# Tile 1's decay sums and exponentials emitted ahead of tile 0's norm, its decays loaded from the input, and a scheduler that keeps column groups apart

## The chip, the cores and the metric

One core of one Trainium2 chip runs the kernel. The metric is the device time of one execution in microseconds (us), median of the runs shown. Names of engines: PE is TensorE (PEld its weight loads), DVE is VectorE, ACT is ScalarE, POOL is GpSimd, SP is SyncE, which here issues most of the DMAs.

## The reference

Three layers follow each other on a batch of 4 sequences of 768 positions. First a decaying state-space attention with 8 heads, computed chunk by chunk:

```python
L = np.exp(cum[:, :, :, None] - cum[:, :, None, :]) * causal   # cum: running sum of log(clip(a))
M = einsum('bhin,bhjn->bhij', Cc, Bc) * L
y = einsum('bhij,bhjd->bhid', M, xc) + einsum('bhin,bhnd->bhid', Cc, state) * exp(cum)
state = exp(sum(la)) * state + sum_j(B_j x_j * exp(cum[-1] - cum))
```

Then an FFN with a norm: `xn = x / sqrt(mean(x*x) + 1e-6) * rms_g`, `(silu(xn @ w_gate) * (xn @ w_val)) @ w_out`, 256 to 1536 to 256. Then a second FFN: each position is mixed with the one before it, `relu(xk @ w_k)**2 @ w_v` times `sigmoid(xr @ w_r)`, 256 to 1024 to 256. The weights arrive as 64-bit floats.

## The kernel before

The sequence is cut into six tiles of 128 positions. A tile holds these positions of all 4 sequences, so its matrices are 512 columns wide (T). The kernel runs a software pipeline over t from 0 to 5: in round t it computes the first FFN of tile t (`ffn1`, twelve units u of 128 hidden columns), the attention of tile t+1 between these units (`attend`), and the second FFN of tile t-1 (`ffn2`). Every large product is three matmuls (lines 670 to 672), a high part and a low part of each operand, so one unit of `ffn1` is 6 matmuls for g, 6 for v and 6 for x.

Weights are converted on the chip. `convert` (from line 246) takes two loaded pieces from a staging tile (`wst`, two buffers) and makes float pairs of them. On DVE that is L265, L270 and L272 on 1024 columns and two subtractions L282; on ACT it is L260, L261 and two casts L281. The pieces come in the order gate, val, out for two units at a time. The conversions for `ffn1` run during round 0, so round 0 has both the matmuls and the conversions.

The attention's decay matrix E exists in two forms. For tiles 0 and 1 it is computed as an exponential: `logs_e` takes the logarithms, `sums_e` (line 340) makes running sums and spreads them over helper operands in the weight tiles `wkh` and `wvvh` (DVE lines 342 to 352), `spread_e` (line 357) makes differences on PE in a PSUM tile Eb (a matmul with `eye`, then one with the sums), and `exp_e` takes exponentials on ACT into E, eight of 512 columns for a tile (E has four buffers, one for each sequence). Later tiles use a scan over decays that were stored to device memory (`la_r`, `la_d`). Independent of that, `la` holds running products of the decays of a tile; `la_scan` (L413) makes them and `ch_mul` (L417) scales C by them. In the kernel before, `decays` writes the clipped decays of all tiles to `la_d`, and `load_la` reads them back for every tile from tile 1.

Before round 0 the code emits: tile 0's sums, exponentials, scores, masks M and outputs y, then the norm of tile 0 (`norm0`: `rms_a` on ACT, `rms_b`, matmuls L646, `xn_f` L652 and `xn_split` L137 and L140), 24 matmuls that keep PE busy (`warm`, L801), the first two conversions, and tile 1's sums. Tile 1's exponentials follow inside round 0, from unit 0, by the table `SCAN`.

The order on each engine is not the emitted one. `Order` (line 998) replays the emitted instructions with a cost table: every engine takes the earliest emitted instruction that is ready, and a tile's buffer has to be free. `arrange` then fixes the resulting order on each engine. Each engine runs its instructions strictly in that order, so an instruction that is not ready holds up those behind it. What counts as ready there depends on `region`, which takes each access as a range of columns.

Of the kernel before, what the change touches and what calls it, by code (L numbers as in the profile page):

```python
# [9 lines left out]
F32 = mybir.dt.float32  # L10
# [6 lines left out]
P = 128  # L17
NB, NH, S, D, N = 4, 8, 768, 32, 16
# [3 lines left out]
T = NB * P  # L22
# [8 lines left out]

SCORES = ((4, 5, 7, 9), (2, 4, 7, 9), (2, 5, 8, 10))
VALUES = ((5, 7, 8, 10), (4, 6, 9, 11), (4, 7, 10, 12))
SCAN = ({0: (0, 1, 2, 3), 3: (4,)}, {0: (0,), 1: (4,), 3: (1,), 5: (2,), 7: (3,)})

NEED = ((6, 6, 6, 10, 10, 12, 12, 14, 16, 16, 18, 18, 18),
        (99, 99, 99, 99, 99, 99, 99, 99, 99, 99, 99, 99, 99))
# [39 lines left out]
def tile_kernel(ctx: ExitStack, tc, a_c, x_t, B_t, B_s, C_s, B_p, C_p, C_h, kc,  # L77
# [110 lines left out]
    def load_a():  # L188
        a_sb = t2("a_sb")[:NC * NR]
        nc.sync.dma_start(out=a_sb, in_=rows4(a_c.rearrange("c r i -> (c r i)")))  # L190
        return a_sb
# [108 lines left out]
    Sf = wp.tile([P, NB, NH // 2, D], F32, name="Sf")  # L300

    def load_la(c):
        t = A[c]["la"] = rp.tile([P, NB, P + 1], F32, tag="la", bufs=2, name="la")
        nc.gpsimd.memset(t[:, :, 0:1], 0.0)
        for b in range(NB):
            nc.sync.dma_start(out=t[:, b, 1:], in_=la_d[c, b].unsqueeze(1).broadcast_to([NH, N, P]))

    def load_ch(c):
        t = A[c]["Ch"] = rp.tile([P, NB, P], F32, tag="Ch", bufs=1, name="Ch")
# [46 lines left out]

    def spread_e(c, b):
        for half in range(2):
            pool, tag = (patt, "at") if c else (pmm, "mm")
            ps = A[c]["Eb", b, half] = pool.tile([P, T], F32, tag=tag, name="Eb")  # L360
            nc.tensor.matmul(ps, eye, before.unsqueeze(1).broadcast_to([P, 4, P]), start=True, stop=False)
            nc.tensor.matmul(ps, spread_l[c][:, 2 * b + half], spread_r[c].rearrange("p h i -> p (h i)"),
                             start=False, stop=True)
# [450 lines left out]
    for _ in range(2):  # L814
        w_load()
    first, second = steps(), steps()
    a_sb = load_a()
    for c in range(2):
        logs_e(c)
    def norm0(s):  # L820
# [5 lines left out]
            xn_split(0, half, s, act_e, vec_e)  # L826

    sums_e(0)
    for b in range(NB):
        spread_e(0, b)  # L830
        for half in range(2):
            exp_e(0, b, half)
    scores(0, 0)
    scores(0, 1)
    for b in range(NB):
        masked(0, b)
        if b + 2 < NB:
            scores(0, b + 2)
        y_mm(0, b)
        y_out(0, b)  # L840
        if b % 2:
            rms_sq(0, cols[b // 2], act_e, vec_e)
            rms_mm(0, cols[b // 2])
        st_up(0, b)
    for s in cols:
        norm0(s)
    warm_up(WARM[1], pacc, "acc")
    for step in first + second:
        step()
    sums_e(1)  # L850
    clip(a_sb)
    decays(a_sb)
    mu_rest()
    carry[0] = rp.tile([P, 2, NB], F32, tag="carry", bufs=2, name="carry")
    nc.vector.memset(carry[0], 0.0)
# [13 lines left out]
    for t in range(NC):  # L869
        c, e = t + 1, t + 2  # L870


        def exps(c, b):
            spread_e(c, b)
            for half in range(2):
                exp_e(c, b, half)

        def late(u):
            for b in SCAN[t].get(u, ()):
                if b == 4:  # L880
                    la_scan(c)
                    ch_mul(c)
                elif c == 1:
                    exps(c, b)
                else:
                    e_scan(c, b)

        def finish(b):
            if b % 2:
                y_two(c, b - 1)  # L890
                for k in range(b - 1, b + 1):
                    if e < NC:
                        load_e(e, k)

        at_sc, at_y = SCORES[min(t, 2)], VALUES[min(t, 2)]

        def attend(u):
            if t <= 1:
                late(u)
            elif u == 0:  # L900
                ch_mul(c)
            if u in (0, 3, 6, 8):
                bc(c, (u + 1) // 3)
            if u in at_sc:
                scores(c, at_sc.index(u))
                masked(c, at_sc.index(u))
            if u in at_y:
                finish(at_y.index(u))
            if u == NU and e < NC:
                load_ch(e)  # L910
                load_x(e)
            if e < NC:
                if u == 4:
                    load_la(e)
                elif u == 7 and t > 1:
                    e_scan(e, 0)
                elif u == 9 and t:
                    la_scan(e)
                elif u == 11 and t > 1:
                    e_scan(e, 1)  # L920
            if t == 0:
                if u == MEANS[0]:
                    rms_sq(c, cols[0], act_e, vec_e)
                if u == MEANS[0] + 1:
                    rms_mm(c, cols[0])
                if u == MEANS[1]:
                    rms_sq(c, cols[1], act_e, vec_e)
                    rms_mm(c, cols[1])
                    rms_a(c, full)

        def hook(kind, u):
            if kind == "ab":
                if t == 0:
                    need(NEED[0][u])
                    if u == 0:
                        for b in range(NB):
                            sf_up(0, b)
                if t == 1:
                    need(NEED[1][u])
                    if u == MIX_UNIT:  # L940
                        mix(0, held.pop(0), act_e, vec_e)
                elif t > 1 and u == 0:
                    mix(t - 1, held.pop(t - 1), act_e, vec_e)
                if c < NC:
                    attend(u)
            if kind == "cd2":
                tail()
            if kind == "cd" and c < NC:
                if t == 1 and u in (1, 2):
                    e_scan(e, u - 1)  # L950
                if u == 0:
                    rms_sq(c, full, act_e, vec_e)
                elif u == 3:
                    rms_mm(c, full)
                    rms_a(c, full)
                elif u == 4:
                    rms_b(c, full)
                    if e < NC:
                        e_scan(e, 2)
                elif u == 5:  # L960
                    xn_out(c, (0,), full, act_e, vec_e)
                    if e < NC:
                        e_scan(e, 3)
                elif u == 6:
                    xn_out(c, (1,), full, act_e, vec_e)

        x2, tail = ffn1(t, hook)
        if t == 0:
            tail()
            hook("ab", NU)  # L970
            rms_b(c, full)
            xn_out(c, range(2), full, act_e, vec_e)
            x2s = quad("x2s", F32).rearrange("p i a n -> p (i a n)")[:, :2 * NB * (P + 1)]
            x2s = x2s.rearrange("p (m b i) -> p m b i", m=2, b=NB)
            nc.gpsimd.memset(x2s[:, :, :, 0:1], 0.0)
            for m in range(2):
                nc.scalar.copy(x2s[:, m, :, 1:], x2[m].rearrange("p (b i) -> p b i", b=NB))
            x2 = [x2s[:, m] for m in range(2)]
        else:
            hook("ab", NU)  # L980
            ffn2(t - 1, hook)
        held[t] = x2
# [22 lines left out]
class Order:  # L1005
    SIGNAL, LANDING, RATE = 90.0, 1900.0, 270.0

    def __init__(self, instructions, slots, chains, groups):
# [13 lines left out]
        self.tiles, self.touch = [[] for _ in range(n)], {}  # L1022
        writes, reads = {}, {}
        for k, i in enumerate(self.ins):
            rs, ws = ([self.region(a, slots) for a in s if hasattr(a, "bass_ap")] for s in (i.ins, i.outs))
            for name in [name for name, _ in rs + ws] + groups.get(i.name, []):
                if name in slots and name not in self.tiles[k]:
                    self.tiles[k].append(name)
                    self.touch.setdefault(name, []).append(k)
            for name, r in rs:  # L1030
                self.meet(k, r, writes.get(name, ()))
            for name, r in ws:
                self.meet(k, r, writes.get(name, ()))
                self.meet(k, r, reads.get(name, ()))
            for store, them in ((writes, ws), (reads, rs)):
                for name, r in them:
                    if slots.get(name, ("",))[0] == "PSUM":
                        store = writes
                    store.setdefault(name, []).append((r, k))
# [1 line left out]


    @staticmethod
    def region(a, slots):
        ap = a.bass_ap
        steps = list(ap.ap)
        row = max(1, steps[0][0])
        at = ap.offset % row
        if ap.tensor.name.startswith("la_") or slots.get(ap.tensor.name, ("",))[0] == "PSUM":
            return ap.tensor.name, (0, 1 << 40, 0, P, None)  # L1050
        end = at + sum((c - 1) * max(s, 0) for s, c in steps[1:]) + 1
        size = 2 if ap.tensor.dtype == BF16 else 4
        return ap.tensor.name, (at * size, end * size, ap.offset // row, ap.offset // row + steps[0][1],
                                at % 2 if steps[-1][0] == 2 else None)

    def meet(self, k, r, others):
        for q, j in others:
# [184 lines left out]
```

## Time and profile before

| | us |
|---|---|
| median of 3 runs | 531.06 (529.59 to 533.97) |
| profiled execution, its time | 531.4 |
| its span, first to last instruction | 529.2 |
| PE busy | 517.0 (98%) |
| DVE busy | 397.5 (75%) |
| ACT busy | 310.3 (59%) |

The profile page has the busy time of each engine and the span in 40 slices of 13.2 us. The views of the trace used below are the stretches (busy time of each engine between two moments, the granted clock of PE and the share of the DMA engines), the waits (who waited for whom), and the timeline (instructions in order of time, equal neighbours merged, with the idle time before them in brackets). Durations in the timeline include the instruction's latency, so neighbours overlap a little; start to start is the rate.

### The profile page before, as it was taken

What the parts mean: (1) busy time and instruction counts of PE and PEld (TensorE: products, weight loads), DVE (VectorE), ACT (ScalarE), POOL (GpSimd) and SP (SyncE); (2) the same over time, 40 slices, a digit from 0 to 9 for tenths busy, and PEclk for the clock granted to TensorE, in tenths of its full rate; (3) what the DMA queues carried; (4) which work ended last, traced back from release to release, by engine and by line L of the source; (5) the groups of instructions that cost most, each with busy time, mean ns of one, the idle gap of its engine ahead of it and who ended that gap; (6) DMA issues with size and microseconds to landing.
All of it is one profiled execution on the core that took longest, in us unless ns stands there. A gap on an engine that the chain in (4) does not pass through costs nothing.

```text
span 529.2 us, 7538 instructions
## 1 busy us (share of the span) xinstructions
PE 517.0 (98%) x2872; PEld 417.4 (79%) x2872; DVE 397.5 (75%) x641; ACT 310.3 (59%) x507; POOL 14.1 (3%) x28
## 2 busy tenths in 40 slices
PE   9968999999999999999999999999999999999997
PEld 5746777888778888888888888788888888888885
DVE  5898999999999686688986587986445863335772
ACT  4768668755747974455874455774437663245552
POOL 4000000000002000001000001000000000000000
PEclk9998999999999999999999999999999999999999
DMA  7837445435334011325011324011000010000001
GB/s 217 276 108 214 170 165 185 154 90 158 111 99 142 19 41 51 109 71 168 20 41 48 112 64 155 2 40 41 0 1 1 0 40 1 1 1 0 22 19 40
DMA packets 21923, 42.34 MB, mean 80 GB/s; under 512 B 2096, under 2 KB 5168, under 8 KB 21888
## 3 DMA queue, kind: packets, MB, share of 16 engines
q1 hardware_dynamic: 19584, 33.48, 19.4%
q10 hardware_dynamic: 2304, 8.39, 4.7%
q8 instruction: 22, 0.36, 0.3%
q14 instruction: 13, 0.11, 0.1%
HBM read 38.52 MB, written 3.34 MB: 79 GB/s over the span
## 4 chain that ended last, share of the span: by engine, by line
PE 69%; DVE 2%; ACT 1%; POOL 0%; ACTq 0%; issue 0%; DVEq 0%
PE v L672 8%; PE v L670 8%; PE v L671 8%; PE g L670 4%; PE x L671 4%; PE x L672 4%; PE x L670 4%; PE g L671 4%; PE g L672 4%; PE kp L670 4%; PE kp L672 4%; PE kp L671 4%; PE y L504 1%; PE sc L472 1%; PE rps L671 1%; PE rps L672 1%
## 5 line engine op out<-in xcount | busy, mean ns | idle before, releaser
L701 DVE TENSOR_TENSOR hf<-sl,v 128x512 f32<-128x512 f32 x72 | 49.1, 682 | 48.9 <-PE v L672 45.7
L137 ACT CAST h<-hf 128x512 fp32r<-128x512 f32 x72 | 44.5, 619 | 65.2 <-DVE hf L701 65.1
L125 ACT ACTIVATE sl<-g 128x512 f32<-128x512 f32 x72 | 42.6, 593 | 44.3 <-PE g L672 44.3
L140 DVE TENSOR_TENSOR h<-hf,h 128x512 fp32r<-128x512 f32 x72 | 50.2, 700 | 23.4 <-ACT h L137 23.3
L670 PE MATMUL g<-xn,wgh 128*128 128x512 f32 x144 | 57.8, 403 | 0.8 <-ACT sl L125 0.8
L670 PE MATMUL v<-xn,wvh 128*128 128x512 f32 x144 | 56.6, 394 | 0.5 <-ACT sl L125 0.5
L671 PE MATMUL g<-xn,wgl 128*128 128x512 f32 x144 | 56.8, 395 | 0.0
L672 PE MATMUL g<-xn,wgh 128*128 128x512 f32 x144 | 56.7, 394 | 0.0
L672 PE MATMUL v<-xn,wvh 128*128 128x512 f32 x144 | 56.4, 392 | 0.0
L671 PE MATMUL v<-xn,wvl 128*128 128x512 f32 x144 | 56.4, 392 | 0.0
L670 PE MATMUL x<-h,woh 128*128 128x512 f32 x144 | 56.2, 390 | 0.0
L671 PE MATMUL x<-h,wol 128*128 128x512 f32 x144 | 56.1, 390 | 0.0
L672 PE MATMUL x<-h,woh 128*128 128x512 f32 x144 | 55.8, 390 | 0.0
L140 DVE TENSOR_TENSOR h<-k,h 128x512 fp32r<-128x512 f32 x48 | 32.8, 685 | 11.6 <-ACT h L137 11.0
L774 DVE TENSOR_TENSOR k<-rl 128x512 f32<-128x512 f32 x40 | 29.7, 748 | 14.7 <-ACT rl L770 14.5
L137 ACT CAST h<-k 128x512 fp32r<-128x512 f32 x48 | 29.8, 621 | 15.8 <-DVE k L774 15.5
L670 PE MATMUL kp<-xm,wkh 128*128 128x512 f32 x96 | 37.7, 393 | 0.0
L672 PE MATMUL v<-h,wvvh 128*128 128x512 f32 x96 | 37.5, 390 | 0.1
L672 PE MATMUL kp<-xm,wkh 128*128 128x512 f32 x96 | 37.4, 390 | 0.0
L670 PE MATMUL v<-h,wvvh 128*128 128x512 f32 x96 | 37.4, 389 | 0.0
L671 PE MATMUL kp<-xm,wkl 128*128 128x512 f32 x96 | 37.3, 389 | 0.0
L671 PE MATMUL v<-h,wvvl 128*128 128x512 f32 x96 | 37.3, 389 | 0.0
(148 smaller groups left out, 1027.8 us busy)
## 6 DMA issues: line engine op xcount, KB each, us to landing
E<-la_r ACTq DMA_DIRECT2D x16, 512.0 KB
x<-in_x_t SPq DMA_DIRECT2D x6, 512.0 KB
wst<-in_w_gate SPq DMA_DIRECT2D x6, 512.0 KB
wst<-in_w_val SPq DMA_DIRECT2D x6, 512.0 KB
wst<-in_w_out SPq DMA_DIRECT2D x6, 512.0 KB
Br<-in_B_s SPq DMA_DIRECT2D x12, 256.0 KB
Cr<-in_C_s SPq DMA_DIRECT2D x12, 256.0 KB
out<-r SPq DMA_DIRECT2D x12, 256.0 KB
```

The source lines that it names most:

```text
L125: ins.append(lambda: nc.scalar.activation(out=out, in_=in_, func=func, **kw))
L137: nc.scalar.copy(x[:, 0, :], src)
L140: last[0] = le.tensor_tensor(out=x[:, 1, :], in0=src, in1=f32(x[:, 0, :]), op=ALU.subtract).ins
L472: nc.tensor.matmul(bank[half][:, q * 256:(q + 1) * 256], bs[:, p, :], cs[:, p, :, :].rearrange("p a i -> p (a i)"), start=True, stop=True)
L504: nc.tensor.matmul(y[half][32 * j:32 * j + 32, at[half]:at[half] + P], x[:, b, h * D:(h + 1) * D], m[:, h, :], start=start and at[half] == ...
L670: nc.tensor.matmul(ps, w[0][:, k, ws], x[:, 0, :], start=first, stop=False)
L671: nc.tensor.matmul(ps, w[1][:, k, ws], x[:, 0, :], start=False, stop=False)
L672: nc.tensor.matmul(ps, w[0][:, k, ws], x[:, 1, :], start=False, stop=last)
L701: nc.vector.tensor_mul(hf, sl, v)
L774: nc.vector.tensor_mul(k2, rl, rl)
```

## The change

Five edits go together. `sums_e(1)` is emitted ahead of tile 0's masks, the exponentials of tile 1 for sequences 0 and 1 ahead of the norm of tile 0, and for 2 and 3 behind the first conversion; their PSUM tiles now come from the pool with four banks. The table `SCAN` loses the entry that placed them in round 0. Tile 1's decays are loaded straight from the input and clipped on DVE (four sequences, 128 columns each); the tile is named `decay` now. The stored decays for the later tiles are loaded, clipped and written in unit 2 of round 0. In the scheduler, `region` becomes `regions`: an access whose outer free dimension has up to 8 separate groups of columns is taken as several ranges.

```diff
-SCAN = ({0: (0, 1, 2, 3), 3: (4,)}, {0: (0,), 1: (4,), 3: (1,), 5: (2,), 7: (3,)})
+SCAN = ({3: (4,)}, {0: (0,), 1: (4,), 3: (1,), 5: (2,), 7: (3,)})
...
-            nc.sync.dma_start(out=t[:, b, 1:], in_=la_d[c, b].unsqueeze(1).broadcast_to([NH, N, P]))
+            src = la_d[c, b] if c > 1 else a_c[c, NH * b:NH * b + NH]
+            nc.sync.dma_start(out=t[:, b, 1:], in_=src.unsqueeze(1).broadcast_to([NH, N, P]))
+        if c == 1:
+            clip(t[:, :, 1:])
...
-            pool, tag = (patt, "at") if c else (pmm, "mm")
-            ps = A[c]["Eb", b, half] = pool.tile([P, T], F32, tag=tag, name="Eb")
+            ps = A[c]["Eb", b, half] = pmm.tile([P, T], F32, tag="mm", name="Eb")
...
-    a_sb = load_a()
...
     scores(0, 0)
     scores(0, 1)
+    sums_e(1)
     for b in range(NB):
         masked(0, b)
...
+    exps(1, 0)
+    exps(1, 1)
     for s in cols:
         norm0(s)
+    for step in first:
+        step()
+    exps(1, 2)
+    exps(1, 3)
     warm_up(WARM[1], pacc, "acc")
-    for step in first + second:
+    for step in second:
         step()
-    sums_e(1)
-    clip(a_sb)
-    decays(a_sb)
...
-                elif c == 1:
-                    exps(c, b)
...
+                if u == 2 and t == 0:
+                    a_sb = load_a()
+                    clip(a_sb)
+                    decays(a_sb)
...
-    def region(a, slots):
+    def regions(a, slots):
...
+        starts, free = [at], steps[1:]
+        inner = sum((c - 1) * max(s, 0) for s, c in free[1:]) + 1
+        if len(free) > 1 and free[0][1] <= 8 and free[0][0] > inner:
+            starts, free = [at + k * free[0][0] for k in range(free[0][1])], free[1:]
```

The first place is PE from tile 0's norm to the first units of round 0. `ss` is the norm's sum and its spread, `Eb` tile 1's differences, g and v are unit 0's products. Before:

```order
L801 MATMUL warm<-ones 128x512
L646 MATMUL ss<-tiny 128x128 x2
L801 MATMUL warm<-ones 128x512 x12
L361 LDWEIGHTS eye
L361 MATMUL Eb<-before,eye 128x512
L670 MATMUL g<-xn,wgh 128x512
...
L672 MATMUL v<-xn,wvh 128x512
L362 MATMUL Eb<-wvvh,wkh 128x512 x2
L670 MATMUL g<-xn,wgh 128x512 x2
```

Now (line numbers are two higher):

```order
L613 MATMUL ss<-ones,sq 128x1 x4
L803 MATMUL warm<-ones 128x512 x2
L363 LDWEIGHTS eye
L363 MATMUL Eb<-before,eye 128x512
L364 MATMUL Eb<-wvvh,wkh 128x512
...
L803 MATMUL warm<-ones 128x512 x4
L648 MATMUL ss<-tiny 128x128 x2
L803 MATMUL warm<-ones 128x512
L648 MATMUL ss<-tiny 128x128 x2
L803 MATMUL warm<-ones 128x512 x15
L672 MATMUL g<-xn,wgh 128x512
```

All eight pairs of Eb matmuls now stand ahead of the last `ss` spread, 15 warm matmuls stand between that and the first g instead of 12, and the first 24 matmuls of g and v (units 0 and 1) have no Eb among them.

The second place is DVE at tile 0's norm. `tiny` is the norm's scalar work, `xnf` and `xn` its result. Before:

```order
L272 SCALAR_TENSOR_TENSOR wt_157<-wt_157,wst_151 128x1024
L566 COPY state<-y 128x64
L632 TENSOR_SCALAR tiny<-ss 128x2
L183 TENSOR_SCALAR a_sb<-a_sb 48x512
L637 SCALAR_TENSOR_TENSOR tiny<-tiny 128x2
...
L272 SCALAR_TENSOR_TENSOR wt_158<-wt_158,wst_154 128x1024
L343 CAST hv<-a_110 128x128
L344 SCALAR_TENSOR_TENSOR hv<-hv,k_sb,a_110 128x128
L352 TENSOR_SCALAR hv<-hv,k_sb 128x128 x2
L347 TENSOR_TENSOR wvvh<-hv,k_sb 128x512
```

Now:

```order
L350 TENSOR_TENSOR wkh<-hv,k_sb 128x768
L493 TENSOR_TENSOR M<-sc,E 128x512 x6
...
L272 SCALAR_TENSOR_TENSOR wt_157<-wt_157,wst_151 128x1024
L183 TENSOR_SCALAR decay<-decay 128x4x128
L572 TENSOR_TENSOR Sf<-state,k_sb 128x128
L415 SCALAR_TENSOR_TENSOR decay<-decay,lmask 128x516
L634 TENSOR_SCALAR tiny<-ss 128x2
L639 SCALAR_TENSOR_TENSOR tiny<-tiny 128x2
L640 SCALAR_TENSOR_TENSOR tiny<-tiny 128x2
L634 TENSOR_SCALAR tiny<-ss 128x2
L419 TENSOR_TENSOR Ch<-Ch,decay 128x512
```

The clip, the scan and the product for tile 1's `decay` now stand ahead of and inside the norm, and tile 1's sums (`hv`, `wvvh`, `wkh`) have gone from behind the second conversion to ahead of tile 0's masks.

The third place is DVE at the end of round 0, where tile 1's norm is finished (`xnf` and `xn` of 512 columns; round 1's g needs them). Before:

```order
L701 TENSOR_TENSOR hf<-sl,v 128x512
L417 TENSOR_TENSOR Ch<-Ch,la 128x512
L701 TENSOR_TENSOR hf<-sl,v 128x512
L282 TENSOR_TENSOR wkl<-wt_1107,wkh 128x2x256
L140 TENSOR_TENSOR h<-hf,h 128x512 x2
L282 TENSOR_TENSOR wkl<-wt_1107,wkh 128x2x256
L652 SCALAR_TENSOR_TENSOR xnf<-yT,k_sb,rb 128x512 x2
```

Now:

```order
L140 TENSOR_TENSOR h<-hf,h 128x512
L703 TENSOR_TENSOR hf<-sl,v 128x512
L282 TENSOR_TENSOR wkl<-wt_1108,wkh 128x2x256 x2
L140 TENSOR_TENSOR h<-hf,h 128x512
L654 SCALAR_TENSOR_TENSOR xnf<-yT,k_sb,rb 128x512 x2
L419 TENSOR_TENSOR Ch<-Ch,decay 128x512
```

The same conversions, units, masks and scans stand ahead of `xnf` in both; only tile 2's product Ch has moved behind it.

## Rows read from the trace of the kernel before

**Rows 1.** The page: busy time, and the span in 40 slices.

```profile
PE 517.0 (98%) x2872; PEld 417.4 (79%) x2872; DVE 397.5 (75%) x641; ACT 310.3 (59%) x507; POOL 14.1 (3%) x28
PEclk9998999999999999999999999999999999999999
```

**Rows 2.** Stretches: from:to, length, busy time (instructions) by engine, PEclk, DMA, GB/s.

```profile
0.00:4.90 4.90, 3.85 (x10) 3.10 (x11) 2.05 (x7) 1.59 (x2) 4.03 (x14) 1.00 0.27 62
0.00:100.47 100.47, 92.59 (x602) 68.91 (x603) 89.24 (x158) 69.38 (x112) 6.17 (x22) 0.98 0.60 195
29.65:100.47 70.82, 64.65 (x384) 48.74 (x383) 67.26 (x105) 51.87 (x78) 0.22 (x2) 0.98 0.55 184
45.00:49.00 4.00, 4.00 (x12) 3.09 (x11) 3.09 (x6) 3.60 (x7) 0.00 (x0) 0.57 0.85 259
103.05:200.00 96.95, 96.39 (x547) 78.38 (x546) 88.58 (x134) 66.30 (x109) 3.56 (x2) 1.00 0.30 92
200.00:524.00 324.00, 323.91 (x1698) 267.26 (x1697) 215.70 (x345) 172.95 (x284) 4.35 (x4) 1.00 0.12 41
```

**Rows 3.** Timeline of PE, 24 to 49 us: start, length, line, operands, idle before.

```profile
24.33 2.98 PE L801 MATMUL warm<-ones 128*128 128x512 f32 x12
27.19 0.58 PE L670 MATMUL g<-xn,wgh 128*128 128x512 f32 x1
32.93 0.73 PE L362 MATMUL Eb<-wvvh,wkh 128*128 128x512 f32 x2 [2.40 <-DVE wkh L347]
34.20 0.39 PE L361 MATMUL Eb<-before,eye 128*128 128x512 bf16 x1
34.67 0.39 PE L361 MATMUL Eb<-before,eye 128*128 128x512 bf16 x1
40.30 0.38 PE L361 MATMUL Eb<-before,eye 128*128 128x512 bf16 x1 [2.48 <-ACT E L125]
42.31 1.61 PE L455 MATMUL sc<-Cr,Br 32*128 32x256 f32 x8 [0.44 <-ACT E L125]
44.70 0.50 PE L670 MATMUL g<-xn,wgh 128*128 128x512 f32 x1 [0.78 <-ACT sl L125]
45.62 0.63 PE L670 MATMUL g<-xn,wgh 128*128 128x512 f32 x1
48.61 0.47 PE L671 MATMUL v<-xn,wvl 128*128 128x512 f32 x1
```

**Rows 4.** Timeline of DVE, 9 to 50 us.

```profile
9.73 1.29 DVE L491 TENSOR_TENSOR M<-sc,E 128x512 f32<-128x512 f32 x2 [1.12 <-ACT E L125]
12.73 0.69 DVE L491 TENSOR_TENSOR M<-sc,E 128x512 f32<-128x512 f32 x1 [1.71 <-PE sc L455]
41.81 1.23 DVE L270 SCALAR_TENSOR_TENSOR wst<-wt,wst 128x1024 int32<-128x1024 int32 x1 [0.67 <-ACT wst L261]
49.42 0.69 DVE L701 TENSOR_TENSOR hf<-sl,v 128x512 f32<-128x512 f32 x1 [1.33 <-PE v L672]
```

**Rows 5.** Timeline of ACT, 19 to 35 us.

```profile
19.40 0.63 ACT L588 ACTIVATE sq<-yT 128x512 f32<-128x512 f32 x1
22.54 0.44 ACT L125 ACTIVATE tiny<-tiny 128x2 f32<-128x2 f32 x2
33.52 1.09 ACT L125 ACTIVATE E<-Eb 128x512 f32<-128x512 f32 x2 [0.54 <-PE Eb L362]
```

**Rows 6.** Tiles la and a_sb: instructions, ns min/median/max.

```profile
L306 SPq DMA_DIRECT2D la<-la_d x20: 574/598/1191, 31.8 to 242.5; - x20
...
L413 DVE TENSOR_TENSOR_SCAN la<-la,lmask x5: 1222/1225/1228, 52.4 to 254.2; 128x516 f32<-128x516 f32 x5
...
L183 DVE TENSOR_SCALAR a_sb<-a_sb x1: 408/408/408, 21.2 to 21.2; 48x512 f32<-48x512 f32 x1
```

**Rows 7.** Stretches: the DMA share around tile 0's norm.

```profile
17.30:21.40 4.10, 3.53 (x59) 2.94 (x49) 4.01 (x9) 3.29 (x9) 0.00 (x0) 1.00 0.93 250
21.40:23.00 1.60, 1.60 (x13) 1.48 (x12) 0.86 (x6) 0.69 (x4) 0.00 (x0) 1.00 0.33 65
```

More of the change, by code (lines that the diff above doesn't have):

```diff
@@ L302, in load_la @@
     def load_la(c):
-        t = A[c]["la"] = rp.tile([P, NB, P + 1], F32, tag="la", bufs=2, name="la")
+        t = A[c]["la"] = rp.tile([P, NB, P + 1], F32, tag="la", bufs=2, name="decay")
         nc.gpsimd.memset(t[:, :, 0:1], 0.0)
         for b in range(NB):
-            nc.sync.dma_start(out=t[:, b, 1:], in_=la_d[c, b].unsqueeze(1).broadcast_to([NH, N, P]))
+            src = la_d[c, b] if c > 1 else a_c[c, NH * b:NH * b + NH]
+            nc.sync.dma_start(out=t[:, b, 1:], in_=src.unsqueeze(1).broadcast_to([NH, N, P]))
+        if c == 1:
+            clip(t[:, :, 1:])
     def load_ch(c):
@@ L828, in tile_kernel, with exps @@
     sums_e(0)
+    def exps(c, b):
+        spread_e(c, b)
+        for half in range(2):
+            exp_e(c, b, half)
     for b in range(NB):
-        spread_e(0, b)
-        for half in range(2):
-            exp_e(0, b, half)
+        exps(0, b)
     scores(0, 0)
     scores(0, 1)
+    sums_e(1)
     for b in range(NB):
@@ L870, in tile_kernel @@
         c, e = t + 1, t + 2
[L873 to L876, printed above, removed]
         def late(u):
@@ L1024, in __init__ @@
         for k, i in enumerate(self.ins):
-            rs, ws = ([self.region(a, slots) for a in s if hasattr(a, "bass_ap")] for s in (i.ins, i.outs))
+            rs, ws = ([r for a in s if hasattr(a, "bass_ap") for r in self.regions(a, slots)] for s in (i.ins, i.outs))
             for name in [name for name, _ in rs + ws] + groups.get(i.name, []):
@@ L1043, in region @@
     @staticmethod
-    def region(a, slots):
+    def regions(a, slots):
         ap = a.bass_ap
-        steps = list(ap.ap)
+        name, steps = ap.tensor.name, list(ap.ap)
         row = max(1, steps[0][0])
         at = ap.offset % row
-        if ap.tensor.name.startswith("la_") or slots.get(ap.tensor.name, ("",))[0] == "PSUM":
-            return ap.tensor.name, (0, 1 << 40, 0, P, None)
-        end = at + sum((c - 1) * max(s, 0) for s, c in steps[1:]) + 1
+        if name.startswith("la_") or slots.get(name, ("",))[0] == "PSUM":
+            return [(name, (0, 1 << 40, 0, P, None))]
         size = 2 if ap.tensor.dtype == BF16 else 4
-        return ap.tensor.name, (at * size, end * size, ap.offset // row, ap.offset // row + steps[0][1],
-                                at % 2 if steps[-1][0] == 2 else None)
+        odd = at % 2 if steps[-1][0] == 2 else None
+        starts, free = [at], steps[1:]
+        inner = sum((c - 1) * max(s, 0) for s, c in free[1:]) + 1
+        if len(free) > 1 and free[0][1] <= 8 and free[0][0] > inner:
+            starts, free = [at + k * free[0][0] for k in range(free[0][1])], free[1:]
+        span = sum((c - 1) * max(s, 0) for s, c in free) + 1
+        rows = ap.offset // row, ap.offset // row + steps[0][1]
+        return [(name, (b * size, (b + span) * size, *rows, odd)) for b in starts]
     def meet(self, k, r, others):
```

## Prediction

> **What bounds the kernel now.** I read the page first: PE is busy for 517.0 of 529.2 us, so a change can only gain where PE waits or runs slowly, or where work leaves PE's path [rows 1]. Then the stretches, to find those places. From 103 to 524 us PE is idle for 0.56 + 0.09 us; all that can be won lies ahead [rows 2]. One digit of the clock line in the page is 8 [rows 1], and the stretch 45 to 49 us shows it: granted clock 0.57 [rows 2]. The timeline of PE there shows four waits: 2.40 us for tile 1's sums, 2.48 and 0.44 us for its exponentials, 0.78 us for a silu [rows 3]. The first is a wait by order: g and v matmuls of units 0 and 1 stand behind an Eb matmul whose sums DVE is still making. Last, DVE: from 29.65 to 100.47 us it is busy for 67.26 of 70.82 us [rows 2]. In round 0 it converts weights and makes the units' h, so it is almost as full as PE. **Two ledgers therefore count, PE's and DVE's, and the smaller gain of the two decides.**
>
> **PE's ledger.** The sums, exponentials and Eb matmuls of tile 1 leave round 0.
> - Waits that go: 2.40 + 2.48 + 0.44 + 0.78 = 6.1 us [rows 3].
> - Slow clock: 7 matmuls from 45.62 to 48.61 us took 0.427 us each; the 12 warm ones of the same shape from 24.33 to 27.19 us took 0.238 [rows 3]. 8 x 0.19 = 1.5 us, which goes if the waits go.
> - Eight Eb pairs: 0.47 us each by 34.20 to 34.67 us [rows 3], 3.8 us. They now run where warm matmuls ran or where PE had to wait for the norm anyway.
> - Later start of g, a loss. The norm's end: ACT finished the second `sq` at about 20.0 us and its tiny work at 23.0 us [rows 5]. Now four exponentials stand between them. Their rate is half of 1.09 us each [rows 5]; the fourth waits for an Eb pair that stands behind `ss` and warm matmuls. I count 2.4 us for the four, then 1.4 us for both column groups' tiny work, from a start 0.3 us earlier (DVE's idle stretch before the masks is filled, so the exponentials of tile 0 start no later): 19.7 + 2.4 + 1.4 = 23.5 to 23.9 us. One more microsecond for DVE's tiny work and the warm matmuls before the second spread gives a spread done at about 26.1 us. Behind it stand 15 warm matmuls at 0.238 us, 3.6 us: g starts at 29.6 to 29.7 us, not 27.19 [rows 3]. Loss 2.4 us.
> - Sum: 6.1 + 1.5 + 3.8 - 2.4 = **9.0 us, the ceiling.**
>
> **DVE's ledger.** Up to `xnf` of tile 1 at 100.47 us, DVE has the same list of work before and now (the third place of the order), so its lead is the idle time that vanishes. Idle before: 100.47 - 89.24 = 11.2 us [rows 2]. What stays:
> - the start up to 4.9 us, 4.90 - 2.05 = 2.85 us [rows 2]; nothing there is moved;
> - the masks. DVE idled 1.12 and 1.71 us there [rows 4]; the sums of tile 1 (about 3.3 us, seven instructions) fill that. From hand-placing the new order I keep 0.4 us between masks, 0.4 us for L261, 0.6 us in the norm: 1.4 us;
> - round 0: 70.82 - 67.26 = 3.56 us before [rows 2]. The wait of 0.67 us for L261 (ACT was busy with exponentials) and of 1.33 us for a v at the slow clock go [rows 4]; 1.56 us stays, and I add 0.25 us, because the second conversion's L260 and L261 now stand behind the last exponentials on ACT: 1.8 us.
>
> 11.2 - 2.85 - 1.4 - 1.8 = 5.2 us. The clip of `decay` has no row of its own shape: 128 partitions by 4 x 128. The lower bound is nothing, if it falls into a wait; the upper, the clip of 48x512, 0.41 us, the same columns [rows 6]; I take 0.41. Ch of tile 2 leaves the list, 0.6 us. The scan (1.22 us) and Ch of tile 1 are on both lists, only earlier [rows 6]. **5.2 - 0.4 + 0.6 = 5.4 us.**
>
> **The loads of `decay`.** SP issues four 64 KB loads behind the second staging tile and one of 96 KB less; la needed 0.6 us of SP each [rows 6], and nothing that is due before 25 us is queued behind them but Ch. By my placing DVE comes to the clip at 21.3 us. The DMA engines are 0.93 busy until 21.4 us and 0.33 until 23 us [rows 7], so the loads, ahead of others in that queue, land between 17 us (no cost) and 23 us (1.7 us, all of it ahead of the norm). I take nothing, since they are in the first half of what is queued. The Trainium skill, "DMA: Bandwidth & Descriptors", section "Bandwidth", rates a 64 KB transfer at 138 GB/s, where the row shows 250 [rows 7]; an estimate by that page makes the four loads 1.9 us long, the upper end of the wait about 2.6 us and the sum 3 us at worst. No row here shows four such loads in a full queue.
>
> **Other edits at nothing.** The stored decays of later tiles move into round 0: two DVE operations of 0.41 us that were there or ahead of it [rows 6]; their readers come tens of us later. The finer regions change order and no work; where DVE and PE stay full the order costs nothing.
>
> **Sum.** The smaller ledger decides: the profiled execution took 531.4 us, less 5.4 is 526.0. Its time is 0.3 us above the median, so I say **525.7 us** against 531.06. From 103 us on the lead stays, because PE runs there without waits and DVE has the same lead.
>
> **The rivals.**
> 1. *DVE's backlog does not bind.* Among DVE's work ahead of `xnf` are conversions of w_k that round 0 does not need; if they let urgent work past, PE's ceiling of 9.0 us comes: 522.1 us. For it: PE has no wait after 50 us before. Against: `wkl` stands ahead of `xnf` in the new order too. Chance 0.15.
> 2. *The waits come back at other conversions.* Only the 2.40 us wait for the sums and the 3.8 us of Eb go, less the 2.4 us late start: 3.8 us, 527.3 us; with the late loads above, 529. For it: unit 2's g still needs the second conversion, which DVE ends near 36 us by my placing, about when PE has run the 24 matmuls of units 0 and 1. Chance 0.24.
> 3. *Slower: the clock falls in units 2 to 6.* If PE starves in pieces at every conversion between 36 and 61 us, the granted clock falls as it did after the four waits [rows 2, 3]. Each matmul then costs 0.19 us more. 28 of them take back the 5.4 us, 56 make it over 1% slower, that is 24 us at the low level of 1.2 GHz where 8 matmuls ran before: about 537 us. Against: PE's slack in round 0 is 9.0 - 5.4 = 3.6 us, less than the 6.1 us that cost 8 matmuls. The Trainium skill, "TensorE: Matmul & The Clock Gate", section "Part 1: The HAM clock gate", says that the low clock is the default and recent activity lifts it; by that the pieces would matter by how they bunch. The trace agrees: 0.57 behind the waits, 1.00 again from 49 us. Chance 0.06.
>
> **How the numbers follow.** A measurement of this kernel tells a change of about 1%, 5.3 us, from none. The forecast has 0.55 (524 to 528 us), and lies at that line: 0.35 of it over 1% faster, 0.2 within. Rival 1 adds 0.15 to faster; rival 2 goes to no change, 0.24; rival 3 to slower, 0.06. Faster 0.5, same 0.44, slower 0.06. The range takes in rival 1 and rival 2 with late loads, 521.7 to 529.8 us.
>
> **What would show it.** In the changed profile: no wait for sums or exponentials in PE's waits; the first g at 29 to 30 us; the first g of round 1 (103.05 us before) at 97 to 98.5 us; DVE idle for under 7 us up to that `xnf`; PEclk without an 8 in its fourth digit. A first g past 31 us, or a wait of DVE for a decay load, would show the loads or the exponentials on the norm's path dearer than I say; a first g of round 1 near 94 us, rival 1.

## The result and the profile after

The changed kernel takes 534.05 us (median of 6 runs, 532.45 to 537.36) against 530.64 us for the one before, timed beside it: ratio 1.0062, 95% interval 1.0033 to 1.0091. It is slower by 0.6%; the forecast was 525.7 us, with 529.8 us as the upper end. The profiled execution took 535.64 us, 1.6 us above its median, of which the span is 533.9 us.

The page of the changed kernel, to be read against [rows 1]:

```profile
PE 519.5 (97%) x2872; PEld 419.3 (79%) x2872; DVE 397.3 (74%) x642; ACT 310.7 (58%) x507; POOL 11.9 (2%) x28
PEclk9999989999889999999999999999999999999999
```

The 8 in the fourth place is gone, as forecast. There are three others, in the sixth, eleventh and twelfth place. The stretches, against [rows 2]:

```profile
0.00:98.92 98.92, 95.10 (x605) 70.76 (x606) 88.43 (x158) 68.64 (x111) 6.24 (x22) 0.98 0.63 199
45.00:49.00 4.00, 4.00 (x19) 3.09 (x19) 3.93 (x6) 1.87 (x4) 0.00 (x0) 1.00 0.04 14
76.00:80.00 4.00, 4.00 (x14) 2.88 (x15) 2.30 (x5) 2.23 (x3) 0.00 (x0) 0.65 0.92 309
100.96:200.00 99.04, 92.51 (x530) 75.56 (x529) 86.83 (x131) 66.63 (x108) 1.39 (x2) 0.97 0.28 88
200.00:529.00 329.00, 328.67 (x1718) 270.89 (x1717) 218.67 (x350) 174.28 (x287) 4.29 (x4) 1.00 0.12 41
```

The first stretch ends at `xnf` of tile 1, at 98.92 instead of 100.47 us. The fourth starts at the first g of round 1, at 100.96 instead of 103.05 us: a lead of 2.1 us. In that stretch PE now idles for 6.53 us (0.56 us before); afterwards for 0.33 us. So the lead is lost in one place. The timeline of PE shows it (start, length, line, operands, idle before):

```profile
32.55 0.39 PE L672 MATMUL g<-xn,wgh 128*128 128x512 f32 x1
74.13 1.05 PE L613 MATMUL ss<-ones,sq 128*128 128x1 f32 x8 [1.41 <-ACT sq L590]
147.63 0.80 PE L672 MATMUL g<-xn,wgh 128*128 128x512 f32 x1 [6.53 <-ACT sl L125]
148.22 0.63 PE L673 MATMUL g<-xn,wgl 128*128 128x512 f32 x1
149.93 0.63 PE L674 MATMUL g<-xn,wgh 128*128 128x512 f32 x1
150.36 0.45 PE L672 MATMUL v<-xn,wvh 128*128 128x512 f32 x1
151.09 0.39 PE L672 MATMUL v<-xn,wvh 128*128 128x512 f32 x1
```

A g waits 6.53 us for a silu. Matmuls that start 0.43 us apart follow, where the later ones start 0.22 us apart: six of them, 1.2 us. The sum, from 2.1 us ahead: 2.1 - (6.5 - 0.6) - 1.2 = 5.0 us behind, and the span is 4.7 us longer (533.9 against 529.2). On ACT, the same moments of the changed kernel:

```profile
129.39 0.59 ACT L125 ACTIVATE sl<-g 128x512 f32<-128x512 f32 x1
141.68 0.66 ACT L260 ACTIVATE wt<-wst 128x512 f32<-128x512 f32 x1 [1.93 <-DMA wst<-in_w_v]
144.39 0.62 ACT L281 CAST wvvh<-wt 128x512 fp32r<-128x512 f32 x1 [1.48 <-DVE wt L272]
144.91 2.17 ACT L137 CAST xm<-xf 128x512 fp32r<-128x512 f32 x4
146.99 0.58 ACT L125 ACTIVATE sl<-g 128x512 f32<-128x512 f32 x1
```

Between two silus lie 17.6 us. The last piece of w_v, issued at 133.06 us, reaches ACT 8.6 us later, and its conversion and the four `xm` casts of the mix (each position mixed with the one before it, for the second FFN) stand ahead of the silu. ACT takes its instructions in order, so the silu waits, g's and v's fill `pmm`, and PE stops. None of this is needed soon: the first matmul kp of the second FFN (`xk @ w_k`), which reads `xm`, runs at 163.41 us, the first matmul on `wvvh` (the converted w_v) at 172.05 us. The kernel before, ACT, same place:

```profile
138.26 0.66 ACT L260 ACTIVATE wt<-wst 128x512 f32<-128x512 f32 x1
138.83 0.66 ACT L261 ACTIVATE wst<-wst 128x512 int32<-128x512 uint32 x1
139.39 0.58 ACT L125 ACTIVATE sl<-g 128x512 f32<-128x512 f32 x1
139.86 1.13 ACT L137 CAST xm<-xf 128x512 fp32r<-128x512 f32 x2
```

There the piece (issued at 132.29 us) was waited for by nobody, and a silu stood ahead of the casts. The theory to test: **the 0.6% were lost in this pile-up, and the scheduler's new rule made it.** The rival: the move itself costs, by the late first g (32.55 us).

### The profile page after: what moved, and what is told of

Read it like the earlier page. It is cut to its first block, busy times and chain, and to the rows that moved or that the text cites. A ratio compares the mean times of both kernels' runs of the same rounds, so it can differ in the third digit from the quotient of the medians.

```text
span 533.9 us, 7552 instructions
## 1 busy us (share of the span) xinstructions
PE 519.5 (97%) x2872; PEld 419.3 (79%) x2872; DVE 397.3 (74%) x642; ACT 310.7 (58%) x507; POOL 11.9 (2%) x28
## 4 chain that ended last, share of the span: by engine, by line
PE 69%; DVE 2%; DMA 2%; ACT 1%; POOL 0%; issue 0%; ACTq 0%; SPq 0%; DVEq 0%
PE v L674 8%; PE v L672 8%; PE v L673 8%; PE g L672 5%; PE g L673 4%; PE g L674 4%; PE x L672 4%; PE x L673 4%; PE x L674 4%; PE kp L672 4%; PE kp L674 4%; PE kp L673 4%; DMA wst<-in_w_v 2%; PE y L506 1%; PE sc L474 1%; PE rps L674 1%
## 5 line engine op out<-in xcount | busy, mean ns | idle before, releaser
L140 DVE TENSOR_TENSOR h<-hf,h 128x512 fp32r<-128x512 f32 x72 | 49.3, 686 | 23.5 <-ACT h L137 23.3
L672 PE MATMUL g<-xn,wgh 128*128 128x512 f32 x144 | 58.6, 407 | 6.5 <-ACT sl L125 6.5
L674 PE MATMUL g<-xn,wgh 128*128 128x512 f32 x144 | 57.1, 397 | 0.0
L424 DVE TENSOR_TENSOR_SCAN E<-E,cmask 128x1024 f32<-128x1024 f32 x16 | 37.3, 2330 | 1.4 <-DMA E<-la_r 1.4
L672 PEld LDWEIGHTS g<-xn,wgh 128*128 128x128 f32 x144 | 27.4, 191 | 13.5 <-ACT sl L125 7.4
```

Of the source, the lines that this page charges most:

```text
L140: last[0] = le.tensor_tensor(out=x[:, 1, :], in0=src, in1=f32(x[:, 0, :]), op=ALU.subtract).ins
L424: nc.vector.tensor_tensor_scan(out=e, data0=e, data1=cmask, initial=0.0, op0=ALU.mult, op1=ALU.max)
L672: nc.tensor.matmul(ps, w[0][:, k, ws], x[:, 0, :], start=first, stop=False)
L674: nc.tensor.matmul(ps, w[0][:, k, ws], x[:, 1, :], start=False, stop=last)
```

## Experiments

Ratios are to the kernel before, run on the same chip; the sets and the last control ran on four different chips. **First set: which part of the change, and which place.**

The mix two units of `ffn1` later, in the changed kernel:

```diff
-SUB_DVE, MIX_UNIT = tuple(range(27)), 7
+SUB_DVE, MIX_UNIT = tuple(range(27)), 9
```

> The changed kernel with one number changed: the mix of tile 0 is emitted at unit 9 of round 1, not 7. Theory A (pile-up): the 0.6% were lost in one place, at 141 us, where the last w_v conversion and the four xm casts stand on ACT ahead of a silu; PE waits 6.53 us there and runs six matmuls at the low clock, about 1.2 us more. With the mix two units later the silus keep their turn, the wait goes, and the lead of 2.1 us at the first g of round 1 (100.96 against 103.05 us) stays: 534.05 - 7.7 = 526.3 us, at most 528.5 if small waits take its place. Theory B (late start): the first g at 32.55 us (27.19 before) is what costs, and the wait at 141 us only shows it: no change, 533 to 535 us. Theory C (deadline moved): the mixed rows then come late for the first kp of tile 0, and PE waits there instead: about 530 us.

Measured: 529.24 us, 0.9973 (0.9953 to 0.9993). The 6.53 us wait is gone, and the time with it, so theory B does not hold. But the gain is 4.8 us, not 7.7. PE's list of waits (us in total, times, longest) shows what took the rest:

```profile
PE y L542 <- DVE E L493: 2.0, 1, 2.0
PE x L674 <- DVE h L140: 1.1, 1, 1.1
```

The w_v piece was still late (issued at 130.30, used at 139.43 us), and DVE stood idle for it with the mask that y needs standing behind its conversion.

Only the scheduler's rule (`regions` for `region`) in the kernel before:

> The kernel before with only the scheduler's new rule (column groups of an access are kept apart); sums, exponentials and decays stand where they stood. Theory A: the new rule alone lets the last w_v conversion and the xm casts pass a silu in round 1, so the same long PE wait (4 to 7 us near 140 us) appears, and with round 0 as before the time is above before: 533 to 538 us. Theory B: the sums and exponentials ahead of the first norm are what costs, the rule changes order and no time: 529 to 531 us, no wait over 1 us in round 1.

Measured: 538.56 us, 1.0155 (1.0127 to 1.0182): theory A, just above its range. The same wait, at the same matmul, with no sums moved:

```profile
149.56 0.80 PE L670 MATMUL g<-xn,wgh 128*128 128x512 f32 x1 [5.93 <-ACT sl L125]
```

The changed kernel with the old rule (`region` for `regions`):

> The changed kernel with the scheduler's old rule; sums, exponentials and decays moved as in the change. Theory A: no wait over 1.5 us in round 1, and the move of the sums gives part of what was forecast: 526 to 529.5 us. Theory B: the move itself costs: 533 to 535 us, with a first g at 31 to 33 us and no lead at the first g of round 1.

Measured: 528.28 us, 0.9945 (0.9928 to 0.9962): theory A. Its first g comes at 32.10 us and its first g of round 1 at 100.95 us, the same lead as in the changed kernel. Here the lead stays: the span is 526.5 us, 2.7 less than before. A late first g therefore doesn't make the kernel slow.

The two runs show the cause from both sides: the rule without the move has the long wait, the move without the rule does not. The parts do not add up, though: +1.55% and -0.55% would give +1.0%, and both together gave +0.62%.

The control, `MIX_UNIT` 9 in the kernel before:

> The kernel before with the mix at unit 9, a control for the first run: before had no pile-up at the mix, so by theory A nothing is to be won, 530.6 us within 1 us. If instead a later mix is a gain of its own, 526 to 528 us, and the first run would show nothing of the change.

Measured: 530.89 us, 0.9996 (0.9983 to 1.0008), as theory A says.

**Second set: why the w_v piece lands late, and whether DVE sets the end of round 0.** The piece goes on ACT's queue, all else in the same order:

```diff
-            nc.sync.dma_start(out=st[:, i]...
+            (nc.scalar if j + i == 26 else nc.sync).dma_start(out=st[:, i]...
```

> The changed kernel with one transfer on another queue: the last w_v piece (512 KB) is issued by ACT, not by SP behind Br and Cr (256 KB each); every other instruction keeps its place. Theory A (two causes in the pile-up: the order, and a load that lands late): in the changed kernel this load took 8.6 us from its issue to ACT's first use, ACT idled 1.93 us and DVE 2.29 us for it. Ahead of Br and Cr, in the kernel before, the same load took about 6 us. If it lands that much sooner, PE's wait of 6.53 us shrinks by 2 to 3 us and the time falls from 534.05 to 531 to 532 us; what stays is the order (four xm casts ahead of a silu). Theory B (the order alone): the wait stays at 6 to 7 us, 533.5 to 535 us.

Measured: 534.35 us, 1.0073 (1.0049 to 1.0097): theory A's cure fails. But the load was not earlier either, so the test doesn't say that an early load is worth nothing:

```profile
133.02 0.42 ACTq L241 DMA_DIRECT2D wst<-in_w_v  x1
142.13 0.66 ACT L260 ACTIVATE wt<-wst 128x512 f32<-128x512 f32 x1 [2.38 <-DMA wst<-in_w_v]
```

That is 9.1 us on a queue of its own. (The 6 us that this expectation reads from the kernel before are an upper bound: nobody waited for the load there.) The mix at unit 9 and the piece on ACT's queue together:

> Mix at unit 9 and the last w_v piece on ACT's queue together. With the mix at unit 9 alone (529.24 us) DVE still idled 3.54 us for this piece and PE then waited 2.04 us for a mask and 1.10 us for an h. Theory A: the earlier landing takes away the 2.04 us and part of the 1.10 us: 526 to 527.5 us. Theory B: those waits come from DVE's own work in that stretch, not from the load: 528.5 to 529.5 us.

Measured: 529.83 us, 0.9978 (0.9961 to 0.9995), no better than the mix alone, and its PE still waits 1.8 us for the mask. Two more scans on DVE in round 0, on top of that:

> The previous kernel with two scans of 128x512 more on DVE in round 0 (about 1.2 us each, results unused), all other instructions in the same order. Theory A, the forecast's ledger: DVE sets the end of round 0, so 2.4 us of work on it move the first g of round 1 and the end by 2 to 2.4 us: about 529 us against 526.7. Theory B: PE sets it, and DVE has slack there: 0 to 0.8 us.

Measured: 531.73 us, 1.0008 (0.9994 to 1.0021): 1.9 us more for 2.44 us of scans (1.218 us each). Nearer to theory A than to B. The medians alone would be weak evidence, as that of the previous kernel takes in executions in which the clock fell near 76 us (below). The profile agrees: the first g of round 1 starts at 100.89 us against 98.21 us with the mix alone, which has the same order up to there without the scans and no fall; 0.76 us of that is a slower start, and 1.9 us are left. In this order, DVE's time in round 0 comes back nearly in full.

One unit later still, `MIX_UNIT` 10:

> Mix at unit 10 and the last w_v piece on ACT's queue. Theory A: once the silus keep their turn, one unit more gives nothing: the same as with unit 9, within 0.7 us. Theory C (deadline): the mixed rows come late for the first kp of tile 0, and PE waits there: 1 to 3 us more than with unit 9.

Measured: 530.39 us, 0.9993 (0.9973 to 1.0012). PE waits 2.5 us for an h instead; a later mix gives nothing.

**Third set: the loads.** The DMA engines in the kernel before, 128 to 148 us, in 40 slices of 0.5 us (busy tenths of 16 engines, GB/s):

```profile
DMA  0099854898898952100302222222222000012222
GB/s 0 0 172 352 344 221 172 336 336 344 287 184 307 332 201 82 33 0 16 33 20 98 98 111 98 86 111 86 102 98 90 16 0 0 0 20 33 102 102 106
```

Br and Cr of tile 3 (rows of the attention's B and C), issued at 135.99 and 136.62 us and alone, move at a flat 100 GB/s. A digit is a tenth cut off; the stretch gives the share as 0.26:

```profile
139.00:142.50 3.50, 3.50 (x17) 2.79 (x15) 3.38 (x7) 3.04 (x6) 0.00 (x0) 1.00 0.26 99
```

The changed kernel, 128 to 144 us, slices of 0.4 us:

```profile
DMA  9799998200002031227699995222222210002402
GB/s 174 256 420 430 399 389 297 113 0 0 0 0 61 20 41 46 102 102 133 143 328 333 225 230 143 77 97 102 102 102 102 102 61 5 0 0 41 20 0 87
```

Br and Cr are now issued ahead of w_v. After the burst near 136 us the same digit 2 and 100 GB/s run on until 141 us, when w_v is done. A share of 0.26 is about that of four of 16 engines at work all the time. The idea to test is that pieces of w_v on those four wait behind Br and Cr whatever the queue. It fits the failed move to ACT's queue, but no view shows the single engines. The Trainium skill, "DMA: Bandwidth & Descriptors", section "Why a DMA increments its semaphore by 16 and not by 1", says that a transfer runs on the largest number of engines, up to 16, that divides the slowest dimension of both sides. Br repeats 32 rows four times, so that dimension is 4; the 0.26 agrees with 4 of 16. The cure would be pieces of 32 rows:

```diff
-                nc.sync.dma_start(out=r, in_=src[c, b].unsqueeze(0).broadcast_to([4, 32, 4 * P]))
+                for g in range(0, P, 32):  # for c = 3, b < 2
+                    nc.sync.dma_start(out=r[g:g + 32], in_=src[c, b])
```

> The changed kernel with the Br and Cr loads of tile 3 (first two sequences) each issued as four transfers of 32 rows instead of one that repeats 32 rows four times. Why: in the kernel before these two loads, alone, moved at a flat 100 GB/s with 0.2 of the DMA engines' time (138 to 143 us), and in the changed kernel the w_v piece that shared their time landed only when that tail ended, on SP's queue (8.6 us) as on ACT's own (9.1 us). Theory A (the tail is in how these loads lie on few DMA engines): in four pieces they move at over 200 GB/s, w_v lands 2 to 3 us sooner, and PE's wait of 6.5 to 7.0 us shrinks by that: 531 to 532.5 us. Theory B (w_v itself is slow here, or the wait is all order): the wait stays, 533.5 to 535 us. In neither case does the wait go, since the order stays.

Measured: 533.63 us, 1.0042 (1.0023 to 1.0060). The profile has the earlier load and the shorter wait of theory A:

```profile
130.68 0.38 SPq L241 DMA_DIRECT2D wst<-in_w_v  x1
135.22 0.68 ACT L260 ACTIVATE wt<-wst 128x512 f32<-128x512 f32 x1 [0.84 <-DMA wst<-in_w_v]
142.84 0.80 PE L672 MATMUL g<-xn,wgh 128*128 128x512 f32 x1 [4.08 <-ACT sl L125]
```

The load takes 4.5 us instead of 8.6 to 9.1, and the wait is 4.08 us instead of 6.53: late load 2.5 us, order 4.1 us. The median doesn't show it: the times are in two groups, 531.3 to 532.7 and 534.6 to 535.0 us, and the interval overlaps that of the changed kernel. In the profile, too, the clock takes part of it back: 13 matmuls behind this wait start some 0.43 us apart, six behind the long one. In this kernel two of Br's four pieces and all of Cr's are also issued behind w_v and not ahead of it, so the split is not the only thing that moved, and what it does alone is not shown.

> Mix at unit 9 with the same split loads. Theory A: the idle 3.5 us of DVE before the w_v conversion shrinks, and with it PE's wait of 2.0 us for a mask: 527 to 528.3 us against 529.2. Theory B: no change, 528.7 to 529.8 us.

Measured: 527.42 us, 0.9933 (0.9910 to 0.9955). Theory A: no wait of y is left, and the median is 1.8 us less than with the mix alone. The two intervals just touch; the profiled spans (523.9 against 526.4 us, neither with a fall of the clock) show the gain more clearly. The times again lie in two groups, 525.6 to 526.2 and 528.7 to 529.1 us.

**Fourth set: a wait that sometimes lets the clock fall.** In the changed kernel, PE waits 1.41 us ahead of the ss matmuls at 74.13 us. Behind it the changed kernel's granted clock was 0.65 from 76 to 80 us, and PE ran 14 matmuls there. The kernel with the mix alone has the same order and the same wait up to there; its stretch:

```profile
76.00:80.00 4.00, 4.00 (x21) 2.84 (x21) 3.88 (x7) 3.28 (x5) 0.00 (x0) 1.00 0.91 323
```

It has 21 matmuls: the fall costs 7 x 0.23 = 1.6 us in this stretch. That is all it costs there: `xnf` of tile 1 starts 2.75 us later in the changed kernel's profile than in this one, of which 1.12 us are a slower start. With the mix at 9 and the piece on ACT's queue the same stretch is at 0.50, wholly at the low level of 1.2 GHz, and by the same sum the fall costs 3.1 us:

```profile
76.00:80.00 4.00, 4.00 (x11) 2.78 (x9) 1.42 (x3) 1.91 (x3) 0.00 (x0) 0.50 0.93 343
```

Of the eight profiles with this wait, the clock fell in four (0.50 to 0.73) and stayed at 1.00 in four. Seven of them have the same work up to there, and they part by the moment at which the ss matmuls start: 73.52, 73.82, 74.11 and 74.13 us where the clock fell, 73.00, 73.40 and 73.42 us where it did not. The moment differs by the slower or faster start. (The eighth, with two more scans, starts them at 75.58 us and kept its clock.) With a fall of 1.6 us behind a start some 1 us slower, two executions of one kernel are about as far apart as the two groups of times above; but no execution of an upper group was profiled, so that this is what parts them is not shown. One constant moves the emission of the sums of squares one unit later; the scheduler then orders round 1 anew as well:

```diff
-MEANS = (7, 10)
+MEANS = (8, 10)
```

> Mix at unit 9, and the sums of squares of tile 1's first half (ss) emitted one unit later. Why: in the changed kernel PE waits 1.41 us for the square ahead of them at 73 to 74 us (not in the kernel before), and in four of the six profiles with the new rule and the move the clock then fell for some 4 us. Theory A: this wait and the fall go, 1.4 us in each execution and about 1.6 us in those that fall: 527 to 528 us, with less scatter. Theory B: DVE sets the end of round 0 in any case: 528.8 to 529.8 us.

Measured: **526.39 us, 0.9916 (0.9902 to 0.9930)**, better than theory A, with all times within 525.8 to 527.6 us. No wait at ss is left and no fall: the mean granted clock is 0.999 or 1.000 in all five executions, as it is in all eleven of the kernel with the old rule and of the next one, which lack the wait too. `xnf` of tile 1 starts at 93.96 us. The stretch up to it, and the stretches up to the first g of round 1 here, with the mix alone and in the kernel before:

```profile
0.00:93.96 93.96, 91.24 (x605) 67.64 (x606) 87.25 (x155) 68.46 (x112) 7.57 (x22) 1.00 0.65 210
0.00:98.04 98.04, 95.32 (x624) 70.39 (x625) 91.33 (x161) 71.03 (x115) 7.57 (x22) 1.00 0.62 201
0.00:98.21 98.21, 94.42 (x624) 70.27 (x624) 90.81 (x161) 69.71 (x114) 7.47 (x22) 1.00 0.61 201
0.00:103.05 103.05, 95.17 (x624) 70.82 (x625) 91.82 (x161) 71.09 (x116) 6.17 (x22) 0.98 0.59 190
```

The gain over the mix alone is not where theory A put it. `xnf` starts 2.2 us earlier, but the first g of round 1 only 0.2 us, behind a start that was 0.4 us faster; PE is busy without a break from `xnf` to that g in both. In this order w_v is issued at 126.58 us, ahead of Br, and ACT uses it 4.7 us later without a wait; the waits of 2.0 and 1.1 us in round 1 are gone with it. So the profile's gain comes from round 1, and the smaller scatter goes with the fall that stays out.

> Mix at unit 9, ss one unit later and split loads together. If all three theories hold: 525 to 526.5 us, the best of all; if the split loads give nothing, the same as without them.

Measured: 527.18 us, 0.9927 (0.9915 to 0.9939): split loads give nothing where w_v is issued ahead of them anyway.

Last, the control for the best kernel, the kernel before with `MIX_UNIT` 9 and `MEANS` (8, 10):

> The kernel before with the mix at unit 9 and the sums of squares of tile 1's first half one unit later, a control for the best kernel (526.39 us). Theory A: before has neither of the two stalls that these constants take away, so they are worth little alone: 529.8 to 530.9 us, and the gain of the best kernel is the change's. Theory B: the constants are a gain of their own: 526 to 528 us.

Measured: 532.89 us, 1.0028 (1.0008 to 1.0049). The constants alone give nothing, they rather cost; the gain of 0.84% comes from the change together with an order freed of its two stalls. How much of it is the new rule's was not run: the old rule with these constants is missing. The traces hint that the rule also gives something: with the old rule the first g of round 1 starts at 100.95 us, with the new one, where the clock does not fall, at 98.0 to 98.6 us.

## Why the prediction was wrong

**The step that failed: "From 103 us on the lead stays, because PE runs there without waits and DVE has the same lead."** It took round 1 to be the same work in the same order. In its place, a lead of 2.1 us was lost in one wait of 6.53 us for a silu near 141 us and in the slow matmuls behind it (1.2 us). It rests on another sentence that failed, under the edits at nothing: "The finer regions change order and no work; where DVE and PE stay full the order costs nothing." The rule alone costs 1.55%, with a wait of 5.93 us at the same matmul. The forecast followed the order up to `xnf` only. In round 1, ACT is not full, so being full doesn't protect; what counts there is what stands ahead of the silu in ACT's order.

**PE's ledger.** The four waits of [rows 3] and the slow matmuls behind them are gone, as forecast (clock 1.00 at 45 to 49 us). The late first g was mis-sized: 5.36 us, not 2.4. Of it 1.24 us are the start: the first 16 warm matmuls took 6.74 us here and 5.50 us in the profile before. The other 4.1 us (in the best kernel's profile too, 31.05 us with an earlier start) are the change's. The forecast had the norm's tiny work done at 23.5 to 23.9 us, and it started only at 25.95 us:

```profile
22.65 1.55 ACT L125 ACTIVATE E<-Eb 128x512 f32<-128x512 f32 x3
25.46 0.60 ACT L125 ACTIVATE E<-Eb 128x512 f32<-128x512 f32 x1 [1.25 <-PE Eb L364]
25.95 0.26 ACT L125 ACTIVATE tiny<-ss,k_sb 128x2 f32<-128x2 f32 x1
```

The masks, too, waited 2.34 us for an exponential, and the second `sq`, behind which these exponentials stand, started at 22.11 us, 2.7 us later than before [rows 5], where the forecast had it 0.3 us earlier. This term doesn't decide the time, as the kernel with the old rule shows.

**DVE's ledger** gave 5.4 us up to `xnf`; the changed kernel shows 1.55, but that execution lost 1.24 us at the start and 1.6 us to the fall of the clock behind the ss wait. The mix and split kernels, the same up to there without the fall, start `xnf` at 96.17, 96.60 and 96.65 us, 3.8 to 4.3 us ahead, and the best kernel 6.5 us ahead with 93.96 - 87.25 = 6.7 us of DVE idle (forecast: under 7). The first g of round 1, forecast at 97 to 98.5 us, comes at 98.04 to 98.64 us in these four profiles. So the size of the lead was near the truth, but that DVE alone sets it is not shown. The two added scans say that DVE's time counts; the best kernel says that an `xnf` 2.2 us earlier than with the mix alone brings the first g 0.2 us. PE's ledger gives the same lead once its terms have their measured size: up to the first g PE idles for 7.88 us before and 3.79 us with the mix alone. The four waits of 6.1 us went, and one of 0.6 us; waits of 1.41, 0.6, 0.4 and 0.3 us, which were in no term, came, the longest of them at ss.

**The `decay` loads at nothing:** right. The clip took 0.42 us at 23.77 us and waited for no load, so the 2.6 us of the prediction's estimate did not come. The 138 GB/s that it takes from the Trainium skill, "DMA: Bandwidth & Descriptors", section "Bandwidth", are given there for transfers issued from GpSimd, and these were issued by SP.

**Rivals.** The third had the right sign and the wrong place: the clock does fall (76 to 80 us), but behind one wait of PE, not through starved conversions in units 2 to 6, and it costs 1.6 us in three profiles and 3.1 us in one. The second's 527.3 to 529 us is near the kernels without the pile-up, for other reasons.

Open: why the scheduler, with the finer rule, puts the silu behind the casts was not followed through its choices. Whether the 1.41 us wait alone lets the clock fall, or its place beside the 128x1 matmuls or the moment at which it comes, wasn't tried either.

## What to carry to other kernels

When a scheduler writes the order, a rule that removes false dependencies is not free: compare the order on each engine to the end of the program, and ask of each in-order queue what stands ahead of the work that frees PSUM. Work that isn't due for 16 us, with a load in front of it, doesn't belong ahead of a silu. Undo each part of a change alone: here one part alone was worth 0.55%, the other alone cost 1.55%, and together they cost 0.62%, so neither number can be read off the whole.

## What the runs showed of the hardware

- Loads that repeat 32 rows four times moved alone at 99 GB/s on 0.26 of the DMA engines' time (kernel before). A 512 KB load issued behind two of them was first used 8.6 us after its issue, and 9.1 us on a queue of its own; issued ahead of them, 4.7 us, and nobody waited for it.
- The same wait of 1.41 us, in the same order of work, let the clock fall in four of eight profiles, at a cost of 1.6 to 3.1 us. Among the seven with equal work, the four that fell are those where it came latest, by as little as 0.1 us; seven are few for a rule.
- The first 16 warm matmuls took 5.25 to 6.74 us across 15 profiles, and what follows them in the start shifts by as much: 1.12 us slower in the changed kernel than with the mix alone, first g 1.12 us later.
